# An attention and gated-MLP block on one core: loads on SP's queue, closing steps on Pool, a bf16 product with gb

## The chip, the cores and the metric

The kernel runs on one core of one Trainium2 chip. The metric is the device time of one execution in microseconds; lower is better. TensorE (PE in the profile, PEld for its weight loads), VectorE (DVE), ScalarE (ACT), GpSimd (POOL) and SyncE (SP) each work through their own list of instructions in the order in which the program gives them; they wait for each other through semaphores. DMA transfers are issued by SP, ACT or Pool.

## The reference

Two blocks with residual connections; 2048 rows, width 512, bf16 inputs.

```
mod = silu(c) @ w_mod                      # six vectors: sa, ca, ga, sb, cb, gb
h   = layernorm(x) * (1 + ca) + sa
x   = x + ga * A(h)
h   = layernorm(x) * (1 + cb) + sb
x   = x + gb * B(h)
```

A is attention: `q = h @ wq` in 32 heads of 128; keys and values come from a cache of 8 heads with 2048 positions, each shared by 4 heads of q; `softmax(q k^T / sqrt(128)) v`, and the heads' results times `wo`. B is a gated MLP: `z = gelu(h @ w_in)`; its second half is normalised by rows and mixed over positions, `g = w_sp @ z2 + b_sp`; the result is `(z1 * g) @ w_out`.

## The kernel before

**Attention.** The work is cut into 128 units (NU): 8 groups, one for each key head, by 16 tiles of 128 rows. A unit is one tile of q against one key head, for 4 heads. Group g, tile j is unit 16 g + j. The program writes the order out by hand: a loop of iterations `it` (L1404), each of 8 slots. Iteration `it` computes the scores of unit `it` (`qk`, L996), the PV products of an earlier unit and, at its end, the output projection (`wo_proj`, L1118) of a still earlier one. `at(it, slot, fn)` (L993) puts any other step in front of a given slot; `fill` holds the matmuls of the q projection for the next block of 4 units (L947). Iterations of the steady part take some 8.7 us.

**Two kinds of units.** From unit 8 to unit 118 every second unit is "by rows" (`by_rows`, L972). In a unit by columns the scores stand with the key positions on the partitions (L1030); ACT's exp (L1037) writes them so that PV can use them at once, in the next iteration (L1086, o_ps). DVE divides by the sums (L1097 and L1098, into onorm), and a DMA transpose on SP turns the result into oT (L1109). In a unit by rows the scores stand the other way (L1011); exp (L1018) writes rows into one of six buffers called pn (three of them lie in win_sb, one in wmod_a), and after each head a DMA transpose of 512 KB on SP turns that head's rows into pT (`turn_rows`, L1047, L1050): the "turns", four in such a unit, the last at slot 0 of the following iteration. PV of a unit by rows follows three iterations later (L1065, with a copy by DVE at L1074).

**The output projection** of a unit by columns runs three or four iterations after its scores (L1143, bank misc) and DVE adds it to the fp32 accumulator of its tile (xacc, L1130); a unit by rows has one matmul, one bank and one scaled addition for each head (L1136). There are two banks each of misc and o_ps; TensorE can only begin to write a bank again when DVE has read it. In the last group (units 112 to 127) each tile is closed: product with ga_rows (L1158), addition to x_sb (L1159), then bn_stats and bn_aggr (`ln_stats`, L696 to L699), all on DVE. The second LayerNorm of the tile follows (`ln2`, L1166): the reciprocal root on Pool (L679, L683), the normalisation on DVE (L687), a transpose on SP (xnT, L1177), the modulation on DVE (hT, L1184).

**Loads.** For each group g the weights wq and wo, the values v and the keys kT are loaded into buffers of which there are two each (`load_wq`, `load_v`, `load_wo`, `load_k`, L720 to L746). The keys go by a DMA transpose on SP. The other three are issued by Pool, at slot 5 of the iteration that follows a unit by rows (L1294 to L1308): in front of each load Pool copies one element of that unit's pT (`after_rows`, L1283), so it waits until the unit's last turn has landed. For group 1 the three loads stand at (5, 0) behind `after_pv(3)`. Pool also issues the rest of w_mod (wmod_b, at (2, 5)), w_in (win_sb, at (126, 4)), and w_out and b_sp at the end of iteration 130 (L1440, L1441). wmod_b is read by `mod_cols_b` (L1197, matmuls at L857) at (4, 4).

**The MLP.** From iteration 128 on, matmuls of z2 (L1321) and z1 (L1360) stand between the last PV products; then come the statistics and the normalisation of z2 on DVE (L1343, L687), the spatial product (L1486) with the w_sp tiles, loaded by DMA transposes on SP (`load_wsp`, L1216), and the product with w_out (L1519). `finish_tile` (L1527) multiplies the result with gb_rows into an fp32 tile tmp (L1531), adds x_sb into yout (L1532), and ACT issues the store (L1533).

Of the kernel before, what the change touches and what calls it, by code (L numbers as in the profile page):

```python
# [10 lines left out]
BF16 = mybir.dt.bfloat16  # L11
FP32 = mybir.dt.float32
ACT = mybir.ActivationFunctionType
ALU = mybir.AluOpType
AX = mybir.AxisListType
P = 128
# [559 lines left out]
def kernel(  # L576
# [19 lines left out]
    nc = tc.nc  # L596
    _, S, D = A_x.shape
    _, HKV, SK, DH = A_k_cache.shape
    HQ = A_wq.shape[1] // DH
    REP = HQ // HKV  # L600
    F = B_w_in.shape[1]
    FH = F // 2
    NMOD = w_mod.shape[1]
    assert DH == P and D == 512 and S % 512 == 0 and SK % 1024 == 0 and FH % P == 0 and REP == 4
    NT = S // P
    NDT = D // P
    NKT = SK // P
    NFT = FH // P
    NCH = S // 512
    CT = 512 // P  # L610
# [11 lines left out]
    v_dram = A_v_cache[0].rearrange("g (t p) d -> p g t d", p=P)  # L622
# [3 lines left out]
    wmod_dram = w_mod.rearrange("(p dt) n -> p dt n", p=P)  # L626
    c_dram = c[0].rearrange("(p j) -> p j", p=P)
    win_dram = B_w_in.rearrange("(dt p) f -> p dt f", p=P)
    wout_dram = B_w_out.rearrange("(ft p) d -> p ft d", p=P)
# [10 lines left out]
    stat = fast.enter_context(tc.tile_pool(name="stat", bufs=2))  # L640
# [7 lines left out]
    ga_rows = res.tile([P, D], FP32, name="ga_rows")  # L648
    gb_rows = res.tile([P, D], FP32, name="gb_rows")
    modc = res.tile([P, 6 * NDT], FP32, name="modc")  # L650
    rall = res.tile([P, NT * HQ], FP32, name="rall")
# [68 lines left out]
    def load_wq(g, engine):  # L720
        wqs[g] = early.tile([P, NDT, REP * DH], BF16, name="wq_g")
        engine.dma_start(
            out=wqs[g][:], in_=wq_dram[:, :, g * REP * DH : (g + 1) * REP * DH]
        )

    def load_v(g):
        v1 = late.tile([P, NKT, DV], BF16, name="v1")
        nc.gpsimd.memset(v1[:, :, DH:DV], 1.0)
        if g > 0:
            nc.gpsimd.dma_start(out=v1[:, :, 0:DH], in_=v_dram[:, g])  # L730
        else:
            nc.sync.dma_start(out=v1[:, 0 : NKT // 2, 0:DH], in_=v_rows)
            nc.sync.dma_start(
                out=v1[:, NKT // 2 : NKT, 0:DH], in_=v_dram[:, 0, NKT // 2 : NKT]
            )
        groups.setdefault(g, {})["v1"] = v1

    def load_wo(g, engine):
        wo_g = late.tile([P, REP, D], BF16, name="wo_g")
        engine.dma_start(out=wo_g[:], in_=wo_dram[:, g * REP : (g + 1) * REP, :])  # L740
        groups[g]["wo"] = wo_g

    def load_k(g):
        kT = early.tile([P, SK], BF16, name="kT")
        nc.sync.dma_start_transpose(out=kT[:], in_=A_k_cache[0, g])
        groups.setdefault(g, {})["kT"] = kT  # L746
# [218 lines left out]
    NU = HKV * NT  # L965
# [27 lines left out]
    def at(it, slot, fn):  # L993
        later.setdefault((it, slot), []).append(fn)
# [123 lines left out]
    def wo_proj(u):  # L1118
        g, j = divmod(u, NT)
        each = by_rows(u)  # L1120
        ps = {}

        def into(first, X_ps, scale):
            if first:
                xaccs[j] = late.tile([P, D], FP32, name=f"xacc{j}", bufs=1)
            xa = xaccs[j]
            if scale is None and first:
                nc.vector.tensor_copy(out=xa[:], in_=X_ps[:])
            elif scale is None:
                nc.vector.tensor_tensor(out=xa[:], in0=X_ps[:], in1=xa[:], op=ALU.add)  # L1130
            elif first:
                nc.vector.tensor_scalar(
                    out=xa[:], in0=X_ps[:], scalar1=scale, scalar2=None, op0=ALU.mult
                )
            else:
                nc.vector.scalar_tensor_tensor(  # L1136
                    out=xa[:], in0=X_ps[:], scalar=scale, in1=xa[:], op0=ALU.mult, op1=ALU.add
                )

        def mm(hh):  # L1140
            if hh == 0 or each:
                ps[0] = bank("misc")
            nc.tensor.matmul(  # L1143
                ps[0][:],
                lhsT=oTs[u][:, hh, :],
                rhs=groups[g]["wo"][:, hh, :],
                start=(hh == 0 or each),
                stop=(hh == REP - 1 or each),
            )
            if each:  # L1150
                c0 = u * REP + hh
                into(g == 0 and hh == 0, ps[0], rall[:, c0 : c0 + 1])
            elif hh == REP - 1:
                into(g == 0, ps[0], None)
            if hh < REP - 1 or g < HKV - 1:
                return
            xa = xaccs[j]
            nc.vector.tensor_tensor(out=xa[:], in0=xa[:], in1=ga_rows[:], op=ALU.mult)  # L1158
            nc.vector.tensor_tensor(  # L1159
                out=x_sb[:, j, :], in0=xa[:], in1=x_sb[:, j, :], op=ALU.add  # L1160
            )
            ln_stats(mv2, j, x_sb[:, j, :])

        return [lambda hh=hh: mm(hh) for hh in range(REP)]
# [89 lines left out]
    ln1_at(1, (0, 7), (1, 2), (2, 2))  # L1254
    ln1_at(2, (2, 4), (3, 1), (4, 5))
    ln1_at(3, (5, 1), (5, 5), (7, 4))
    at(2, 5, lambda: nc.gpsimd.dma_start(out=wmod_b, in_=wmod_dram[:, :, 2 * D : NMOD]))
    at(NU - 2, 4, lambda: nc.gpsimd.dma_start(out=win_sb, in_=win_dram))
    at(4, 4, mod_cols_b)
    at(5, 4, mod_rows)  # L1260

# [18 lines left out]
    at(NU + 1, 0, wsp0)  # L1280
    for st in range(NT):
        at(NU + 1 + st // 4, 2 * (st % 4), lambda st=st: load_wsp(wsp[0], 0, st))
    def after_rows(u):  # L1283

        seen = stat.tile([1, 1], BF16, name="seen")
        nc.gpsimd.tensor_copy(out=seen[:], in_=pTs[u][0:1, NKT - 1, 511:512])

    def after_pv(u):
        seen = stat.tile([1, 1], FP32, name="seen")
        nc.gpsimd.tensor_copy(out=seen[:], in_=rall[0:1, u * REP : u * REP + 1])  # L1290

    at(5, 0, lambda: after_pv(3))
    pauses = [u for u in row_units if not by_rows(u + 1)]
    for g in range(1, HKV):  # L1294
        it = (g - 1) * NT
        loads = (
            (0, lambda g=g: load_wq(g, nc.gpsimd)),
            (4, lambda g=g: load_v(g)),
            (6, lambda g=g: load_wo(g, nc.gpsimd)),
        )  # L1300
        last = it - 1
        for from_it, load in loads:
            if g == 1:
                at(5, 0, load)
                continue
            last = next(u for u in pauses if u >= it + from_it and u > last)
            at(last + 1, 5, lambda u=last: after_rows(u))
            at(last + 1, 5, load)  # L1308
        last = next(u for u in pauses if u >= it + 8 and u > last)
        at(last + 1, 1, lambda g=g: load_k(g))  # L1310


    zs = {}
# [90 lines left out]
    for it in range(NU + 6):  # L1404
        if it < NU:
            if it % CT == 0 and it // CT + 1 < NB:
                set_fill(it // CT + 1)
        elif it == NU:
            free_a.close()
            z2p = fast.enter_context(tc.tile_pool(name="z2p", bufs=1))  # L1410
            zs["z2"] = z2p.tile([P, NT, FH], BF16, name="z2")
        pvs = [u for u in range(max(it - 5, 0), min(it, NU)) if pv_at(u) == it]
        wos = [u for u in range(max(it - 8, 0), min(it, NU)) if wo_at(u) == it]
        wf = [fn for u in wos for fn in wo_proj(u)]
        for i in range(NSLOT):
            for fn in later.pop((it, i), []):
                fn()
            if it < NU:
                qk(it, i)
            if len(pvs) == 1:  # L1420
                pv_part(pvs[0], i, NSLOT)
            elif pvs:
                n = NSLOT // 2
                pv_part(pvs[i // n], i % n, n)
            for fn in fill.pop((it, i), []):
                fn()
            if i >= NSLOT - len(wf):
                wf[i - NSLOT + len(wf)]()
            if it >= NU:
                zrun(3)  # L1430
        for u in wos:
            if u >= (HKV - 1) * NT:
                ln2(it, u % NT)
        if it == NU + 2:
            free_b.close()
            mlp = fast.enter_context(tc.tile_pool(name="mlp", bufs=1, side="right"))
            zs["z1T"] = mlp.tile([P, NFT, S], BF16, name="z1T")
            wout_sb = mlp.tile([P, NFT, D], BF16, name="wout_sb")
            bsp_bc = mlp.tile([P, S], BF16, name="bsp_bc")
            nc.gpsimd.dma_start(out=wout_sb[:], in_=wout_dram)  # L1440
            nc.gpsimd.dma_start(out=bsp_bc[:], in_=B_b_sp.partition_broadcast(P))  # L1441
    assert not later and not fill
    for t in range(1, 3):
        wsp[t] = mlp.tile([P, NT, 512], BF16, name=f"wsp{t}")
# [81 lines left out]

    def finish_tile(t, jj, src):  # L1527
        j = t * CT + jj
        tmp = mlp.tile([P, D], FP32, name="tmp", bufs=2)
        yout = mlp.tile([P, D], BF16, name="yout", bufs=2)  # L1530
        nc.vector.tensor_tensor(out=tmp[:], in0=src, in1=gb_rows[:], op=ALU.mult)  # L1531
        nc.vector.tensor_tensor(out=yout[:], in0=tmp[:], in1=x_sb[:, j, :], op=ALU.add)  # L1532
        nc.scalar.dma_start(out=out_dram[:, j, :], in_=yout[:])  # L1533
# [84 lines left out]
```

## Time and profile before

| | us |
|---|---|
| three runs: median (lowest, highest) | 1313.51 (1313.09, 1313.7) |
| profiled execution: time | 1314.1 |
| profiled execution: span, first to last instruction | 1312.2 |
| PE busy | 1302.6 |
| ACT busy | 1111.5 |
| DVE busy | 629.5 |
| POOL busy | 55.3 |

The profile is of one execution. Its span is 1.9 us shorter than its time, and its time is 0.6 us above the median of the three runs. The granted TensorE clock was 0.999. In lists of waits the columns are: the waiting engine, line and tile, what it waited for, the total in us, how often, and the longest. In a chain and in a timeline the columns are the start in us from the start of the span, the length in us, engine, line and tile; xN stands for N merged instructions. In the table of stretches there follow, after the length, the busy time of PE, PEld, DVE, ACT and POOL with their counts, the granted clock, the share of the DMA engines and GB/s.

### The profile page before, as it was taken

To read this page: it belongs to the slowest core of one execution; us is meant where nothing else is said; L and a number is where in the kernel's file an instruction comes from. 1 tells how busy PE (TensorE), PEld (TensorE's weight loads), DVE (VectorE), ACT (ScalarE), POOL (GpSimd) and SP (SyncE) were. 2 spreads that over 40 slices of the span, in tenths; PEclk is the share of its full clock that TensorE was granted. 3 is DMA by queue.
4 is the path that set the end of the run, shared out by engine and by line. 5 is a ranking of instruction groups with operands and counts; after the bars stand their busy time and mean duration, and the time that the engine had idled before them with its cause. 6 is when DMAs were issued, how large, how long until landed. Compare 5 with 4: busy or idle time off the path is not lost.

```text
span 1312.2 us, 24106 instructions
## 1 busy us (share of the span) xinstructions
PE 1302.6 (99%) x9671; PEld 742.9 (57%) x9671; DVE 629.5 (48%) x1610; ACT 1111.5 (85%) x1509; POOL 55.3 (4%) x116
## 2 busy tenths in 40 slices
PE   9999999999999999999999999999999999999998
PEld 5665555555555555555555555555555566644445
DVE  6532444444444444444444444444444568794444
ACT  7899999999999999999999999999999988650000
POOL 1200000000000000000000000000000001120000
PEclk9999999999999999999999999999999999999999
DMA  7778878777888788787977787778876631464300
GB/s 181 152 103 153 133 141 154 137 132 140 165 154 137 141 142 156 118 145 148 167 140 130 141 158 138 129 139 168 153 137 129 115 55 30 114 139 101 74 17 31
DMA packets 584392, 168.54 MB, mean 128 GB/s; under 512 B 573936, under 2 KB 580336, under 8 KB 584272
## 3 DMA queue, kind: packets, MB, share of 16 engines
q1 hardware_dynamic: 577248, 147.77, 64.3%
q0 software_dynamic: 4432, 16.91, 4.2%
q10 hardware_dynamic: 2592, 2.23, 0.5%
q8 instruction: 78, 1.28, 0.4%
q14 instruction: 42, 0.34, 0.1%
HBM read 21.89 MB, written 2.10 MB: 18 GB/s over the span
## 4 chain that ended last, share of the span: by engine, by line
PE 97%; DMA 1%; DVE 1%; issue 0%; POOL 0%; ACT 0%; DVEq 0%
PE o_ps L1086 19%; PE s_ps L1030 18%; PE s_ps L1011 15%; PE o_ps L1065 15%; PE misc L1143 8%; PE misc L947 8%; PE misc L1486 7%; PE s_ps L1321 2%; PE s_ps L1360 2%; PE o_ps L1519 1%; DMA wsp<-in_w_mod_dram 1%; PE o_ps L788 1%; PE s_ps L1519 0%; DMA hT<-xn 0%; DVE bnst L698 0%; DVE hT L816 0%
## 5 line engine op out<-in xcount | busy, mean ns | idle before, releaser
L1037 ACT ACTIVATE pT<-s_ps 128x1024 bf16<-128x1024 f32 x552 | 561.4, 1025 | 34.6 <-PE s_ps L1030 12.3
L1086 PEld LDWEIGHTS <-pT 128*128 128x128 bf16 x4416 | 295.6, 98 | 129.8
L1030 PE MATMUL s_ps<-qT,kT 128*128 128x512 bf16 x1152 | 342.4, 379 | 0.3 <-ACT pT L1037 0.2
L1086 PE MATMUL o_ps<-v,pT 128*128 128x129 bf16 x4416 | 340.4, 220 | 0.0
L1011 PE MATMUL s_ps<-kT,qT 128*128 128x512 bf16 x896 | 266.5, 379 | 0.0
L1018 ACT ACTIVATE win_sb<-s_ps 128x1024 bf16<-128x1024 f32 x226 | 231.4, 1025 | 3.6 <-ACT win_sb L1018 0.3
L1143 PE MATMUL misc<-wo_g,oT 128*128 128x512 bf16 x512 | 194.0, 379 | 1.1 <-DVE xacc L1136 1.1
L947 PE MATMUL misc<-hT,wq_g 128*128 128x512 bf16 (+2 forms) x520 | 187.0, 371 | 0.1
L1030 PEld LDWEIGHTS <-kT 128*128 128x128 bf16 x1152 | 111.7, 98 | 115.4 <-issue 3.0
L1136 DVE SCALAR_TENSOR_TENSOR xacc<-misc,rall,xacc 128x512 f32<-128x512 f32 x220 | 163.7, 744 | 19.4 <-PE misc L1143 14.4
L958 DVE CAST qT<-misc 128x512 bf16<-128x512 f32 x125 | 85.7, 686 | 162.4 <-PE misc L947 162.4
L1018 ACT ACTIVATE pn<-s_ps 128x1024 bf16<-128x1024 f32 x148 | 151.5, 1025 | 1.6
L1065 PEld LDWEIGHTS <-v 128*128 128x128 bf16 x896 | 87.6, 98 | 105.8
L1065 PE MATMUL o_ps<-wsp,v 128*128 128x512 bf16 x448 | 133.2, 379 | 0.0
L1065 PE MATMUL o_ps<-pT,v 128*128 128x512 bf16 x448 | 132.6, 379 | 0.0
L1074 DVE CAST oT<-o_ps 128x512 bf16<-128x512 f32 x56 | 38.7, 692 | 191.5 <-PE o_ps L1065 191.5
L1011 PEld LDWEIGHTS <-qT 128*128 128x128 bf16 x896 | 87.5, 98 | 58.7
L1486 PE MATMUL misc<-wsp,z 128*128 128x512 bf16 (+2 forms) x560 | 100.7, 336 | 0.0
L1054 DVE TENSOR_TENSOR tot<-rs 128x1 f32<-128x1 f32 x224 | 34.2, 153 | 94.4 <-ACT win_sb L1018 63.0
L1486 PEld LDWEIGHTS <-z 128*128 128x128 bf16 x560 | 50.6, 98 | 48.7 <-issue 0.2
L1018 ACT ACTIVATE wmod_a<-s_ps 128x1024 bf16<-128x1024 f32 x74 | 75.8, 1025 | 0.0
L1097 DVE RECIPROCAL rall<-o_ps 128x2 f32<-128x2 f32 x144 | 24.5, 170 | 105.1 <-PE o_ps L1086 97.8
(113 smaller groups left out, 795.9 us busy)
## 6 DMA issues: line engine op xcount, KB each, us to landing
wq_g<-in_A_wq_dram POOLq DMA_DIRECT2D x7, 512.0 KB, 3.7
v<-in_A_v_cache_dram POOLq DMA_DIRECT2D x7, 512.0 KB, 5.5
wo_g<-in_A_wo_dram POOLq DMA_DIRECT2D x7, 512.0 KB, 4.3
wsp<-in_w_mod_dram POOLq DMA_DIRECT2D x1, 2048.0 KB, 11.8
out_dram<-yout ACTq DMA_DIRECT2D x16, 128.0 KB, 1.7
win_sb<-in_B_w_in_dram POOLq DMA_DIRECT2D x1, 1792.0 KB, 7.9
x_sb<-in_A_x_dram SPq DMA_DIRECT2D x3, 512.0 KB, 5.6
oT<-onorm SPq DMA_TRANSPOSE x72, 2.7
```

Of the source, the lines that this page charges most:

```text
L947: nc.tensor.matmul(ps[0][:, o0 : o0 + n], lhsT=wqs[g][:, dt, hh * DH : (hh + 1) * DH], rhs=hTs[ch][:, dt, c0 : c0 + n], start=(dt == 0), s ...
L958: nc.vector.tensor_copy(out=dst, in_=src)
L1011: nc.tensor.matmul(s_ps[:, c * 512 : (c + 1) * 512], lhsT=qTs[b][:, hh, jj * P : (jj + 1) * P], rhs=groups[g]["kT"][:, k0 : k0 + 512], sta ...
L1018: nc.scalar.activation(out=rows_of(u, hh)[:, half * HK : (half + 1) * HK], in_=s_ps[:], func=ACT.Exp, scale=inv_sqrt_dh, accum_out=rsums[u ...
L1030: nc.tensor.matmul(s_ps[:, h * 512 : (h + 1) * 512].rearrange("p (r q) -> p r q", r=REP), lhsT=groups[g]["kT"][:, kt * P : (kt + 1) * P], ...
L1037: nc.scalar.activation(out=pTs[u][:, 2 * i : 2 * i + 2, :], in_=s_ps[:].rearrange("p (k q) -> p k q", k=2), func=ACT.Exp, scale=inv_sqrt_dh,)
L1065: nc.tensor.matmul(o_pss[u][:], lhsT=groups[g]["v1"][:, kt, 0:DH], rhs=pTs[u][:, kt, :], start=(kt == 0), stop=(kt == NKT - 1),)
L1074: nc.vector.tensor_copy(out=oTs[u][:], in_=o_pss[u][:].rearrange("p (r q) -> p r q", r=REP))
L1086: nc.tensor.matmul(o_ps[:, hh % 2, 0 : DH + 1], lhsT=pTs[u][:, kt, hh * P : (hh + 1) * P], rhs=groups[g]["v1"][:, kt, 0 : DH + 1], start=( ...
L1136: nc.vector.scalar_tensor_tensor(out=xa[:], in0=X_ps[:], scalar=scale, in1=xa[:], op0=ALU.mult, op1=ALU.add)
L1143: nc.tensor.matmul(ps[0][:], lhsT=oTs[u][:, hh, :], rhs=groups[g]["wo"][:, hh, :], start=(hh == 0 or each), stop=(hh == REP - 1 or each),)
L1486: nc.tensor.matmul(g_pss[f][:, :n], lhsT=z2[:, st, f * P : (f + 1) * P], rhs=wsp[t][:, st, c0 : c0 + n], start=(st == 0), stop=(st == NT - ...
```

## The change

- The loads of wq, v and wo for groups 1 to 7 are issued by SP, at slot 1 of the iteration after a unit by rows, without the copies on Pool (`after_rows` and `after_pv` are gone). For group 1 they stand at (6, 2). The keys keep their place.
- wmod_b goes to SP at (1, 4) instead of Pool at (2, 5); win_sb to SP at (TURN_B + 1, 2), which is (120, 2), instead of Pool at (126, 4); w_out and b_sp to SP at the same place as before.
- For tiles 0 to 11 of the last group the product with ga_rows and the addition to x_sb run on Pool. `ln_stats` stays on DVE behind them.
- tmp in `finish_tile` is written and read as bf16, in the same memory.

```diff
-            nc.gpsimd.dma_start(out=v1[:, :, 0:DH], in_=v_dram[:, g])
+            nc.sync.dma_start(out=v1[:, :, 0:DH], in_=v_dram[:, g])
...
             xa = xaccs[j]
-            nc.vector.tensor_tensor(out=xa[:], in0=xa[:], in1=ga_rows[:], op=ALU.mult)
-            nc.vector.tensor_tensor(
+            engine = nc.gpsimd if j < NT - CT else nc.vector
+            engine.tensor_tensor(out=xa[:], in0=xa[:], in1=ga_rows[:], op=ALU.mult)
+            engine.tensor_tensor(
                 out=x_sb[:, j, :], in0=xa[:], in1=x_sb[:, j, :], op=ALU.add
             )
             ln_stats(mv2, j, x_sb[:, j, :])
...
-    at(2, 5, lambda: nc.gpsimd.dma_start(out=wmod_b, in_=wmod_dram[:, :, 2 * D : NMOD]))
-    at(NU - 2, 4, lambda: nc.gpsimd.dma_start(out=win_sb, in_=win_dram))
+    at(1, 4, lambda: nc.sync.dma_start(out=wmod_b, in_=wmod_dram[:, :, 2 * D : NMOD]))
+    at(TURN_B + 1, 2, lambda: nc.sync.dma_start(out=win_sb, in_=win_dram))
...
-    at(5, 0, lambda: after_pv(3))
     pauses = [u for u in row_units if not by_rows(u + 1)]
     for g in range(1, HKV):
         it = (g - 1) * NT
         loads = (
-            (0, lambda g=g: load_wq(g, nc.gpsimd)),
+            (0, lambda g=g: load_wq(g, nc.sync)),
             (4, lambda g=g: load_v(g)),
-            (6, lambda g=g: load_wo(g, nc.gpsimd)),
+            (6, lambda g=g: load_wo(g, nc.sync)),
+            (8, lambda g=g: load_k(g)),
         )
         last = it - 1
         for from_it, load in loads:
-            if g == 1:
-                at(5, 0, load)
+            if g == 1 and from_it < 8:
+                at(6, 2, load)
                 continue
             last = next(u for u in pauses if u >= it + from_it and u > last)
-            at(last + 1, 5, lambda u=last: after_rows(u))
-            at(last + 1, 5, load)
-        last = next(u for u in pauses if u >= it + 8 and u > last)
-        at(last + 1, 1, lambda g=g: load_k(g))
+            at(last + 1, 1, load)
...
-            nc.gpsimd.dma_start(out=wout_sb[:], in_=wout_dram)
-            nc.gpsimd.dma_start(out=bsp_bc[:], in_=B_b_sp.partition_broadcast(P))
+            nc.sync.dma_start(out=wout_sb[:], in_=wout_dram)
+            nc.sync.dma_start(out=bsp_bc[:], in_=B_b_sp.partition_broadcast(P))
...
-        tmp = mlp.tile([P, D], FP32, name="tmp", bufs=2)
+        tmp = mlp.tile([P, D], FP32, name="tmp", bufs=2)[:].bitcast(BF16)[:, 0:D]
```

More of the change, by code (lines that the diff above doesn't have):

```diff
@@ L1282 @@
         at(NU + 1 + st // 4, 2 * (st % 4), lambda st=st: load_wsp(wsp[0], 0, st))
[L1283 to L1290, printed above, removed]
-    at(5, 0, lambda: after_pv(3))
     pauses = [u for u in row_units if not by_rows(u + 1)]
```

## The prediction

> **What bounds the kernel.** I read the page first (busy shares and slices), then who waited for whom on TensorE, then the table of 20 us stretches, then the chain and the timelines where TensorE is not full.
>
> ```profile
> PE 1302.6 (99%) x9671; PEld 742.9 (57%) x9671; DVE 629.5 (48%) x1610; ACT 1111.5 (85%) x1509; POOL 55.3 (4%) x116
> ...
> PE   9999999999999999999999999999999999999998
> ```
>
> A busy PE is not yet PE at its peak, so I looked at its pace as well. In the chain a pair of units repeats every 17.44 us (169.33, 186.77, 204.21), each pair of 512-column matmuls takes 0.43 us and eight of 129 columns 0.45 us, and from 140 to 1080 us the starts in the timeline follow each other at that pace, without a gap. What TensorE waits for by name is nearly nothing:
>
> ```profile
> PE o_ps L788 <- DVE onorm L769: 1.2, 1, 1.2
> PE misc L1143 <- DVE xacc L1136: 1.1, 1, 1.1
> PE misc L857 <- DMA wsp<-in_w_mod_dram: 0.8, 1, 0.8
> ```
>
> So the change, which leaves every matmul as it is, can win only three things: the wait at L857 (0.9 us by the start times: the matmul before it starts at 47.99, L857 at 48.96), the wait at L1143 (1.1 us, near 1098), and the tail behind the last matmul. Loss has no such limit: whatever makes TensorE wait is added in full.
>
> **1. Loads on SP's queue: wmod_b, −0.9.** Today Pool issues it at 37.08, behind its LayerNorm steps, and it lands 11.83 us later, after L857 wants it. At slot (1, 4) on SP it stands behind four hT transposes, whose issue ends at 29.2. With the same 11.8 us it lands at 41, 7 us before 47.99. Behind it stand the first two oT transposes, issued from 29.26; 12 us late they land near 44, and L1143 first reads one at 50.66. So the 0.9 us go, and nothing is late next.
>
> **2. Loads on SP's queue: the three of each group, 0.** They move from slot 5, behind a copy that waited for the unit's last turn, to slot 1 of the same iteration, where SP has just issued that turn.
>
> ```profile
> 157.88 4.54 SPq L1050 DMA_TRANSPOSE wsp<-win_sb  x2
> 162.52 1.56 SPq L1109 DMA_TRANSPOSE oT<-onorm  x1
> 169.41 1.97 SPq L1050 DMA_TRANSPOSE pT<-win_sb  x1
> ```
>
> SP is free from 164.1 to 169.4. A load of 512 KB lands in 3.7 to 5.5 us (page, part 6). SP's own issue of it: 0.52 us for L740's wo; v has 256-byte pieces, and L733, with half as many, took 2.05 us, so some 4 us. It fits the gap, or makes the next turn a microsecond late. A turn feeds its PV only from the third iteration on, some 10 us after its own landing, so that cover takes all of it. The buffers are long free: v of group g−2 is last read four iterations before v of g is loaded, its wo three, its wq more, so SP doesn't wait for them. The removed copies and the Pool issues lie on an engine 4% busy and hid nothing. For group 1, three loads at (6, 2), near 64 us, stand in front of oT transposes read two iterations (17 us) later; at 5 us each that costs nothing.
>
> **3. win_sb, wout and bsp on SP, 0 (at most 1 to 3).** win_sb goes out near 1058; L1321 reads it at 1129.9 without a gap today, so earlier wins nothing. Its 8 us lie ahead of one xnT transpose (1061.94), whose reader on DVE runs at 1072.3. wout and bsp wait on SP for DVE's last closing (Pool issued them at 1154.83), and behind them stand three wsp transposes and the last xnT. That one went out at 1157.83 and DVE waited for it until 1163.79; I estimate 2 us more, from 1 to 1.5 us of issue and the 6.5 us of wout ahead. DVE then works without a break to 1186.97, and is wanted again at 1190.32: 3.3 us of cover.
>
> **4. bf16 product with gb, −0.3.** Only the last tile counts: the last matmul ends at 1306.2, then 0.69 (L1531), 0.69 (L1532), and the store. The first reads PSUM and keeps its 0.69. The second becomes all bf16; L1514 (gb times z1T, 128x512, all bf16) takes 425 ns instead of 692. 0.27 us go.
>
> **5. Closing steps on Pool, +2.2.** For tiles 0 to 11 the product with ga_rows and the addition (L1158, L1159) move to Pool, but bn_stats (L698), the next instruction in DVE's order, reads their result. So DVE is not relieved: it stands still while Pool works, and everything behind (qT casts, the adding of misc banks, onorm) stands with it. Today, at the place where TensorE waits:
>
> ```profile
> 1095.27 0.61 DVE xacc L1130
> ...
> 1095.90 0.70 DVE xacc L1158
> ...
> 1096.63 0.70 DVE x_sb L1159
> ...
> 1097.36 0.70 DVE bnst L698
> ...
> 1098.27 0.65 DVE xacc L1136
> ...
> 1098.95 0.38 PE misc L1143
> ```
>
> From the end of L1130 (1095.87) to bn_stats are 1.49 us. On Pool it is 2P + 0.2, with P for one operation and 0.2 for the handovers (0.09 from DVE to Pool, 0.08 between two Pool operations, 0.03 back, all from the rstd rows).
>
> No row shows P. The nearest on Pool:
>
> ```profile
> 0.24 0.10 POOL L1602 MEMSET const-float32-0.0<- 128x1 f32 x1 [0.24 <-issue]
> ...
> 0.76 0.20 POOL masks.py:197 MEMSET ident<- 128x128 bf16 x1
> 1.04 0.29 POOL masks.py:199 TENSOR_SCALAR_AFFINE_SELECT ident<-ident 128x128 bf16<-128x128 bf16 x1
> ```
>
> A column written costs 0.8 ns (0.20 less 0.10 over 127), and with one operand read 1.5. By the same step two operands give 2.2 ns, 512 columns 1.2 us. That is my value. Lower end: memset's slope alone, 0.5 us. Upper end: the power at L683 costs 0.156 us a column (128x4 1.04, 128x1 0.58), which would be 80 us; a product is no power, so I stop at twice the slope of the one-operand row, 1.6 us.
>
> The Trainium skill (GPSIMD Engine Reference, "Performance versus the Vector engine") says that a two-input elementwise operation is about twice as slow there as on VectorE, 4497 against 2293 ns for 2048 fp32. An estimate from it for 512 is 1.12 us; the stalls below would then be 1.1 us and the whole sum −0.1. No Pool row here can test it.
>
> With P = 1.2 each closing holds DVE 2.6 instead of 1.49 us: 1.1 later. What that costs is read from DVE's idle time before TensorE rewrites the bank in question:
>
> ```profile
> 1060.00:1080.00 20.00, 20.00 (x185) 12.78 (x183) 13.83 (x33) 15.40 (x16) 1.36 (x3) 1.00 0.18 27
> 1080.00:1100.00 20.00, 18.95 (x193) 12.80 (x191) 15.90 (x38) 17.49 (x18) 2.38 (x6) 1.00 0.15 27
> 1100.00:1120.00 20.00, 20.00 (x207) 13.74 (x205) 18.99 (x49) 18.87 (x20) 4.21 (x9) 1.00 0.18 35
> ```
>
> (After the stretch's length come PE, PEld, DVE, ACT and POOL; DVE is busy 13.83, 15.90 and 18.99 of 20 us.) Followed closing by closing:
> - Units 113, 115, 117: DVE idles 0.48, 0.72, 0.78 us before L1097, so 0.6, 0.4, 0.3 are left, against slacks of 0.64, 0.44, 0.44 us at the row unit's L1136 behind. They just fit: 0.1. Units 112, 114, 116 have 2 to 4 us.
> - Unit 119 (the fence above): TensorE already waits, so all of it is added: 1.1.
> - Units 118, 120, 121, 122 and 123 follow while DVE is full: five times 1.1, less 0.2 to 0.7 of idle, against 3.4 to 4.2 us from onorm (L1098) to the next use of that o_ps bank. 0.3, 0.2 and 0.4 stick out at 1117.5, 1122 and 1129.5. DVE is level again at 1138, where it idled 2.5.
>
> Sum 2.1 to 2.2. By P: 0.7 at 1.0, 0.9 at 1.1, 2.2 at 1.2, 3.9 at 1.3, 7.5 at 1.5; −0.3 at 0.5.
>
> **Sum.** −0.9 − 0.3 + 2.2 = +1.0 on the profiled execution: its span 1312.2 becomes 1313.2, its time 1314.1 becomes 1315.1. It is 0.6 above the median of the three runs; on that median, 1313.5, the forecast is 1314.5. About 0.2% (2.6 us) is what a measurement can tell from no change, so this is "within".
>
> **Rivals.**
> - *DVE becomes the bound* (slower). Same mechanism, P of 1.3 or more: from there the stalls are 3.9, the sum passes +2.7, and each further 0.1 us of P costs 1.8. At 1.4: 1318.0. For it: the fixed cost of a Pool operation with a column operand is 0.23 (L679), not 0.10, and the second has mixed types. Against it: the slope above. Chance 0.25.
> - *SP's queue becomes a wait*: wout and bsp make the last xnT over 3.3 us late, or a load pushes a turn past its 10 us of cover. Price, at 5 us late, 1.7 us once: 1316.2; three late loads in each of 7 groups at 0.3 us: 1320. For it: SP's q1 carries 64.3% already. Against: the gaps above. Chance 0.1, half of it over the bound.
> - *Pool is cheap* (P from 0.5 to 1.0): the stalls are −0.3 to 0.7 and the sum −1.5 to −0.5: 1312 to 1313. Chance 0.2, within the bound.
> - *The kernel is faster by over 2.6*: all that TensorE waits from 20 us on adds to some 3 us, a third of it where ACT is full (80 to 130). It would need a gain that I don't see. Chance 0.05.
> - The forecast itself (P from 1.0 to 1.3, queues silent): 0.4.
>
> Faster 0.05, within 0.65, slower 0.30. The range reaches from the cheap Pool, 1312.2, to P = 1.4, 1318.0.
>
> **What would show it.** Pool rows at L1158 and L1159's new places near 1.2 us, and DVE's bn_stats waiting for Pool 12 times; L1143's wait near 1098 at 2.2 instead of 1.1; new waits of L1086 on onorm between 1115 and 1135; no L857 wait; the last yout at 0.43. TensorE still without a gap from 140 to 1030. The prediction fails if a gap stands there, if the first mm of the spatial stage waits for DVE, or if P is outside 1.0 to 1.3.

## The result, and the profile after

The changed kernel takes 1315.95 us (median of 15 runs, 1315.6 to 1316.64) against 1313.51 (15 runs, 1312.62 to 1314.39): ratio 1.0019, 95% interval 1.0011 to 1.0027, so 1.4 to 3.5 us slower. The interval leaves out "no change", and the forecast of +1.0 lies below it. The time lies inside the predicted range and the ratio just inside the 0.2% that the prediction counts as "within"; its value was 1.45 us low. The profiled execution of after took 1315.95 us with a span of 1313.8, 1.6 more than the span before.

The lines of the page that answer to those shown of before:

```profile
PE 1303.2 (99%) x9671; PEld 743.0 (57%) x9671; DVE 606.4 (46%) x1586; ACT 1111.4 (85%) x1509; POOL 59.0 (4%) x96
...
PE   9999999999999999999999999999999999999998
...
q1 hardware_dynamic: 601200, 164.16, 69.2%
```

DVE lost 23 us of work (mostly the 24 operations that went to Pool, and some 4 us by step 4) and the kernel became slower: DVE's busy time was not what counted. What TensorE waits for by name (the list of waits, TensorE's lines):

```profile
PE misc L1143 <- DVE xacc L1136: 2.2, 1, 2.2
PE o_ps L788 <- DVE onorm L769: 1.2, 1, 1.2
PE s_ps L1030 <- ACT pT L1037: 1.0, 2, 0.7
PE o_ps L1086 <- DVE onorm L1098: 0.4, 2, 0.3
```

L1143's wait has doubled, L857's is gone, and two kinds are new or larger: L1086 behind onorm (forecast) and L1030 behind ACT's exp (not forecast). I then put the starts of all matmuls of both traces side by side and took as lost what lies between two starts above the usual pace. The place of a gap is the last start before it. In us of the span:

| stretch | before | after | where |
|---|---|---|---|
| 0 to 20 | 4.4 | 4.6 | start of the program |
| 20 to 60 | 0.9 | 0 | L857, at 48 |
| 60 to 80 | 0 | 0.9 | L1030, at 71.5 |
| 80 to 140 | 1.3 | 1.3 | the same places |
| 140 to 1040 | 0 | 0 | |
| 1040 to 1160 | 1.2 | 3.3 | after, at 1098: 2.34; 1118.6: 0.42; 1123.5: 0.23; 1131.2: 0.35 |
| last matmul's start to the end | 6.4 | 5.7 | tail |

The differences add to 0.2 − 0.9 + 0.9 + 2.1 − 0.7 = 1.6; the spans differ by 1.6.

The largest item is the closing step. The two new groups on Pool (shapes kept apart; busy us and mean ns behind the first bar):

```profile
L1159 POOL TENSOR_TENSOR xacc<-xacc,ga_rows 128x512 f32<-128x512 f32 x12 | 15.2, 1269 | 218.4 <-DVE xacc L1130 201.5 <-DVE xacc L1136 16.9
L1160 POOL TENSOR_TENSOR x_sb<-xacc,x_sb 128x512 bf16<-128x512 f32 x12 | 13.9, 1156 | 0.9
```

And the chain at the place that the prediction showed (start, length, what):

```profile
1095.50 0.61 DVE xacc L1130
1096.10 0.07 issue
1096.17 1.28 POOL xacc L1159
1097.45 0.07 issue
1097.52 1.16 POOL x_sb L1160
1098.68 0.02 issue
1098.71 0.71 DVE bnst L698
1099.41 0.02 issue
1099.44 0.18 DVE mv L699
1099.62 0.65 DVE xacc L1136
```

From the end of L1130 to bn_stats are 2.6 us instead of 1.49; L1136, which frees the bank for L1143, comes 1.1 us later. The list of waits counts DVE's standing still:

```profile
DVE bnst L698 <- POOL x_sb L1160: 31.4, 12, 2.6
```

The stretches show the same from above (length; then PE, PEld, DVE, ACT, POOL):

```profile
1060.00:1080.00 20.00, 20.00 (x184) 12.81 (x183) 11.55 (x30) 15.40 (x16) 5.43 (x9) 1.00 0.34 95
1080.00:1100.00 20.00, 18.13 (x185) 12.35 (x184) 12.00 (x32) 17.44 (x18) 7.72 (x10) 1.00 0.14 27
1100.00:1120.00 20.00, 19.43 (x196) 13.24 (x196) 11.52 (x32) 17.79 (x18) 9.50 (x12) 1.00 0.11 22
```

DVE's busy time falls from 15.90 to 12.00 and from 18.99 to 11.52, and TensorE's falls with it, from 18.95 to 18.13 and from 20.00 to 19.43. A part of the fall is the work that went to Pool; but DVE also stands behind Pool, 2.6 us in each closing, so a lower busy share here does not mean room.

SP's queue carries the group loads without harm to the turns. SP's timeline of after, at the place that the prediction showed:

```profile
157.86 4.82 SPq L1050 DMA_TRANSPOSE wsp<-win_sb  x2
162.77 1.24 SPq L1109 DMA_TRANSPOSE oT<-onorm  x1
164.06 0.57 SPq L722 DMA_DIRECT2D wq_g<-in_A_wq_dram  x1
169.64 1.70 SPq L1050 DMA_TRANSPOSE pT<-win_sb  x1
```

### The profile page after: what moved, and what is told of

It is laid out like the page before. It is cut to its first block, busy times and chain, and to the rows that moved or that the text cites. A ratio compares the mean times of both kernels' runs of the same rounds, so it can differ in the third digit from the quotient of the medians.

```text
span 1313.8 us, 24042 instructions
## 1 busy us (share of the span) xinstructions
PE 1303.2 (99%) x9671; PEld 743.0 (57%) x9671; DVE 606.4 (46%) x1586; ACT 1111.4 (85%) x1509; POOL 59.0 (4%) x96
## 4 chain that ended last, share of the span: by engine, by line
PE 97%; DVE 1%; POOL 1%; issue 0%; ACT 0%; DVEq 0%; POOLq 0%
PE o_ps L1086 19%; PE s_ps L1030 18%; PE s_ps L1011 15%; PE o_ps L1065 15%; PE misc L947 8%; PE misc L1143 8%; PE misc L1475 7%; PE s_ps L1310 2%; PE s_ps L1349 2%; PE o_ps L1508 1%; PE o_ps L788 1%; POOL xacc L1159 0%; PE s_ps L1508 0%; POOL x_sb L1160 0%; DVE bnst L698 0%
## 5 line engine op out<-in xcount | busy, mean ns | idle before, releaser
L1086 PEld LDWEIGHTS <-pT 128*128 128x128 bf16 x4416 | 295.6, 98 | 130.5 <-issue 1.0
L1030 PE MATMUL s_ps<-qT,kT 128*128 128x512 bf16 x1152 | 342.4, 379 | 1.1 <-ACT pT L1037 1.0
L1086 PE MATMUL o_ps<-v,pT 128*128 128x129 bf16 x4416 | 340.4, 220 | 0.4 <-DVE onorm L1098 0.4
L1143 PE MATMUL misc<-wo_g,oT 128*128 128x512 bf16 x512 | 194.0, 379 | 2.2 <-DVE xacc L1136 2.2
L1030 PEld LDWEIGHTS <-kT 128*128 128x128 bf16 x1152 | 111.6, 98 | 117.4 <-issue 5.2
L1136 DVE SCALAR_TENSOR_TENSOR xacc<-misc,rall,xacc 128x512 f32<-128x512 f32 x220 | 163.5, 743 | 19.6 <-PE misc L1143 14.6
```

The source lines that it names most:

```text
L1030: nc.tensor.matmul(s_ps[:, h * 512 : (h + 1) * 512].rearrange("p (r q) -> p r q", r=REP), lhsT=groups[g]["kT"][:, kt * P : (kt + 1) * P], ...
L1086: nc.tensor.matmul(o_ps[:, hh % 2, 0 : DH + 1], lhsT=pTs[u][:, kt, hh * P : (hh + 1) * P], rhs=groups[g]["v1"][:, kt, 0 : DH + 1], start=( ...
L1136: nc.vector.scalar_tensor_tensor(out=xa[:], in0=X_ps[:], scalar=scale, in1=xa[:], op0=ALU.mult, op1=ALU.add)
L1143: nc.tensor.matmul(ps[0][:], lhsT=oTs[u][:, hh, :], rhs=groups[g]["wo"][:, hh, :], start=(hh == 0 or each), stop=(hh == REP - 1 or each),)
```

## The experiments

Every edit is shown against the kernel that it starts from. Ratios are to the kernel before on the same chip, with 95% intervals; its medians there were 1313.19 to 1314.2 us. "Gap" is the excess of one start-to-start distance of matmuls over their pace.

**closings_only: before, with step 5 alone.**

```diff
-            nc.vector.tensor_tensor(out=xa[:], in0=xa[:], in1=ga_rows[:], op=ALU.mult)
-            nc.vector.tensor_tensor(
+            engine = nc.gpsimd if j < NT - CT else nc.vector
+            engine.tensor_tensor(out=xa[:], in0=xa[:], in1=ga_rows[:], op=ALU.mult)
+            engine.tensor_tensor(
```

> The kernel before with one edit: the closing steps of tiles 0 to 11 on Pool. My theory (DVE stands still behind bn_stats): all of the slowdown is here. +2.1 us over before, L1143's wait near 1098 at 2.2 to 2.3 us instead of 1.1, some 1.0 us of waits for o_ps between 1115 and 1135, no other new gap on TensorE. Rival A (the loads on SP's queue cost, Pool's closing is hidden by the banks): within 0.5 us of before.

Measured: 1317.28 us, ratio 1.0030 (1.0018 to 1.0043), +3.8 us: more than the whole change. The gaps of after are all there, to 0.02 us (2.34, 0.42, 0.24, 0.35), and one more, of 1.67 us at 1131.5. Pool's issue of w_in in the kernel before, and then, of this kernel, Pool's timeline and what waits at 1133:

```profile
1118.88 0.83 POOL L1258 DMA_DIRECT2D win_sb<-in_B_w_in_dram  x1 [0.19 <-ACT wsp L1037]
...
1119.21 1.26 POOL L1159 TENSOR_TENSOR xacc<-xacc,ga_rows 128x512 f32<-128x512 f32 x1 [3.67 <-DVE xacc L1130]
1120.55 1.16 POOL L1160 TENSOR_TENSOR x_sb<-xacc,x_sb 128x512 bf16<-128x512 f32 x1
...
1123.80 0.83 POOL L1259 DMA_DIRECT2D win_sb<-in_B_w_in_dram  x1 [0.19 <-issue]
...
1133.20 0.74 PE L1322 MATMUL s_ps<-win_sb,hT 128*128 128x448 bf16 x3 [1.51 <-DMA win_sb<-in_B_w_in_dram]
```

The load now stands behind two closings and the reciprocal roots that wait for them, and goes out 4.9 us later, and the first matmul of z2 (L1322 here) waits for it. So in this change SP's early issue of win_sb is worth 1.7 us, because step 5 makes Pool late.

**loads_only: after, with the closing steps back on DVE** (steps 1 to 4 alone).

```diff
-            engine = nc.gpsimd if j < NT - CT else nc.vector
-            engine.tensor_tensor(out=xa[:], in0=xa[:], in1=ga_rows[:], op=ALU.mult)
-            engine.tensor_tensor(
+            nc.vector.tensor_tensor(out=xa[:], in0=xa[:], in1=ga_rows[:], op=ALU.mult)
+            nc.vector.tensor_tensor(
```

> The changed kernel with the closing steps back on DVE: the moved loads and the bf16 product alone. My theory: -1.2 us against before (the wait at L857, 0.9, and 0.3 in the tail), waits at 1098 as before (1.1). Rival A (the loads on SP's queue cost something that the profile of the changed kernel shows as 0.9 us without a named cause at 71.5 us, while group 1's three loads are in flight): that gap is here again and the time is -0.3 us. Rival B (the gap belongs to one execution): it is not here.

Measured: 1313.49 us, ratio 1.0000 (0.9991 to 1.0009). No wait at L857, the gap at 1098 is 1.21 as in before, the tail 5.7, and a gap of 1.53 us at 71.4 takes the gain away. The forecast −1.2 did not come: something in steps 1 to 4 costs about what they win.

**stats_later: after, with bn_stats of tiles 0 to 11 at slot 2 of the next iteration**, so that other work of DVE can stand in front of it.

```diff
-            ln_stats(mv2, j, x_sb[:, j, :])
+            if j >= NT - CT:
+                ln_stats(mv2, j, x_sb[:, j, :])
...
-        at(it + 1, 0, first)
-        at(it + 1, 4, second)
+        if j < NT - CT:
+            at(it + 1, 2, lambda: ln_stats(mv2, j, x_sb[:, j, :]))
+            at(it + 1, 3, first)
+            at(it + 1, 6, second)
+        else:
+            at(it + 1, 0, first)
+            at(it + 1, 4, second)
```

> The changed kernel with bn_stats and bn_aggr of tiles 0 to 11 two slots into the next iteration, so that DVE has other work while Pool closes a tile; the steps behind them move with them (rstd to slot 3, normalisation to slot 6). My theory: the same Pool operations cost nothing once DVE does not stand behind them; all waits of TensorE between 1040 and 1140 go, also the 1.1 us of the kernel before. -2.3 us against before, some -4.5 against the changed kernel. Rival (Pool's operations slow DVE by themselves, through a shared way to the memory, or the delayed LayerNorm is late for z2): no gain, or DVE's operations beside Pool's are longer than 0.69 us (1136: longer than 0.74).

Measured: 1311.98 us, ratio 0.9989 (0.9980 to 0.9998), 4.0 us below after. From 1040 to 1160 one gap of 0.14 us is left; the kernel before's own 1.21 us at 1098 is gone with the others. Pool does the same 24 operations for the same time. The rival, Pool slowing DVE by itself, holds for one kind of operation: L1136 beside Pool takes 0.75 us as elsewhere, but four of the modulations (hT, 0.30 us elsewhere) last 1.15 to 1.27 us, each beginning 0.05 to 0.11 us behind a Pool operation and ending 0.05 us behind it. TensorE loses nothing there. And DVE has not stopped standing behind Pool:

```profile
DVE bnst L698 <- POOL x_sb L1160: 22.3, 10, 2.6
```

In ten of the twelve closings bn_stats still waits for Pool, 22.3 us in all instead of 31.4 in after. In the first six hardly anything of DVE's stands between, and DVE idles 2.3 to 2.6 us as in after; TensorE waited for none of this in after either. Near 1098 two of L1136 now come first and bn_stats waits only 0.7 us, and in the five closings after that DVE stands 6.2 us instead of 13.1. So the edit did not end the standing; it took it away where TensorE waited for what stands behind bn_stats.

**third_pool_op: after, with a third operation of the same size on Pool in each closing**, a sum into a tile that nobody reads.

```diff
+            if j < NT - CT:
+                junk = late.tile([P, D], BF16, name="junk", bufs=1)
+                engine.tensor_tensor(out=junk[:], in0=xa[:], in1=x_sb[:, j, :], op=ALU.add)
```

> The changed kernel with one more Pool operation of the same size in each closing of tiles 0 to 11 (a sum into a tile that nobody reads), between the two. By the bookkeeping of DVE's idle time and slack, a closing of 3.9 instead of 2.6 us costs 13 us over before, 11 over the changed kernel: now units 113, 115 and 117 stick out too, 1.6 to 2 us each. Rival (only unit 119, where TensorE already waits, counts): +1.2 us over the changed kernel.

Measured: 1327.17 us, ratio 1.0103 (1.0088 to 1.0119); 11.2 us above after, for 12 operations of 1.16 us. Its waits of TensorE:

```profile
PE o_ps L1086 <- DVE onorm L1098: 4.7, 3, 2.0
PE misc L1143 <- DVE xacc L1136: 3.8, 3, 3.4
PE misc L1143 <- DVE qT L958: 2.1, 3, 0.9
```

The slack that swallowed the first 1.1 us in the early units is used up: TensorE now waits at three places there too, but 1.1 to 1.2 us each, where 1.6 to 2 were expected of units 113, 115 and 117. What TensorE loses from 1040 to 1160 adds to 14.9 us instead of 3.3, which is 11.6 more for a dose of 13.9 us. Not all of it is waiting: TensorE stands still 3.57 us at L1143, up to 1104.74, and the granted clock is 0.50 from 1103.5 to 1110.3 us, where matmuls of 512 columns start 0.43 us apart instead of 0.21. That costs 2.7 of the 14.9 us; the waits add to 12.2, 8.9 more than in after. In no other run does the clock fall between the first 8 us and the tail.

**wmod_only: before, with step 1 alone.**

```diff
-    at(2, 5, lambda: nc.gpsimd.dma_start(out=wmod_b, in_=wmod_dram[:, :, 2 * D : NMOD]))
+    at(1, 4, lambda: nc.sync.dma_start(out=wmod_b, in_=wmod_dram[:, :, 2 * D : NMOD]))
```

> The kernel before, with wmod_b alone issued by SP at slot (1, 4) instead of by Pool at (2, 5). Theory (step 1 of the prediction stands by itself): the gap of 0.9 us at L857 is gone, nothing else is late, 0.9 us less than before. Rival (the gap near 71 us is only L857's gap come back later, in whatever kernel loses the wait at L857): L857 runs without a wait and a gap of about 0.9 us stands near 71 us at L1030, though group 1's loads are still on Pool; 0.0 us.

Measured: 1313.06 us, ratio 0.9998 (0.9989 to 1.0007). No wait at L857 near 48 us and no gap near 71, so the rival (L857's gap come back) fell. But 0.9 us are not won by the medians either: 0.1 us less, and the interval reaches from 1.4 less to 0.9 more, so it does not exclude them.

**group1_only: before, with group 1's three loads alone on SP at (6, 2)**, and without Pool's copy in front of them.

```diff
-            nc.gpsimd.dma_start(out=v1[:, :, 0:DH], in_=v_dram[:, g])
+            (nc.sync if g == 1 else nc.gpsimd).dma_start(out=v1[:, :, 0:DH], in_=v_dram[:, g])
...
-    at(5, 0, lambda: after_pv(3))
...
-            (0, lambda g=g: load_wq(g, nc.gpsimd)),
+            (0, lambda g=g: load_wq(g, nc.sync if g == 1 else nc.gpsimd)),
...
-            (6, lambda g=g: load_wo(g, nc.gpsimd)),
+            (6, lambda g=g: load_wo(g, nc.sync if g == 1 else nc.gpsimd)),
...
-                at(5, 0, load)
+                at(6, 2, load)
```

> The kernel before, with group 1's three loads alone (wq, v, wo) issued by SP at (6, 2), and the copy on Pool that waited for the third unit left out. Theory (these loads at this place delay ACT's exp near 71 us by themselves): the gap of 0.9 us at L857 stays and one of 0.9 to 1.5 us stands near 71 us; 0.9 to 1.5 us more than before. Rival (the gap near 71 us is L857's come back): L857's gap stays, none near 71 us; 0.0 us.

Measured: 1314.07 us, ratio 1.0007 (0.9998 to 1.0016). The gap near 71 us is there, 0.54 us at 70.7, though nothing else of the change is in this kernel. Its size is below the expected 0.9, and the median's +0.9 is not told from zero. Moving the loads brings the gap without any other part of the change; and the theory's other half, that L857's gap stays, failed: L857 did not wait at 48 us in this execution, with wmod_b on Pool as in before.

**bf16_only: before, with step 4 alone.**

```diff
-        tmp = mlp.tile([P, D], FP32, name="tmp", bufs=2)
+        tmp = mlp.tile([P, D], FP32, name="tmp", bufs=2)[:].bitcast(BF16)[:, 0:D]
```

> The kernel before, with the product with gb kept in bf16 alone. Theory (step 4): the last addition takes 0.42 instead of 0.69 us, the span 0.3 us less. Rival (the tail of 6.4 us became 5.7 in every kernel with the whole change, so more than the addition is shorter): 0.7 us less, with the store's way to the end 0.4 us shorter too.

Measured: 1313.48 us, ratio 1.0002 (0.9993 to 1.0011), too small to be seen in the time. The last addition takes 0.43 us instead of 0.69. The tail is 6.35 us against 6.4, and the two kernels above, which lack this step, have 6.0 and 6.5: the store's end scatters by more than the step is worth, so the tail's −0.7 in after is not all step 4's.

**group1_later and group1_pool: loads_only, with group 1's loads elsewhere**, spread over three later iterations on SP, or on Pool at (5, 0) as before.

```diff
-            if g == 1 and from_it < 8:
-                at(6, 2, load)
+            if g == 1:
+                at(*{0: (9, 2), 4: (11, 1), 6: (13, 1), 8: (9, 1)}[from_it], load)
```

> The kernel of loads_only (moved loads and bf16 product, closing steps on DVE) with group 1's three loads still on SP, but one at a time behind units by rows, at (9, 2), (11, 1) and (13, 1), as the other groups have them. loads_only stands still at 71.4 us (L1030, 1.5 us) while three loads follow each other in SP's queue. Theory (three loads at once, in the stage in which the fill of the LayerNorm and of the mod rows is still going on, hold up the queue and what TensorE and ACT exchange): the gap goes, -1.3 against loads_only and before, no gap at the new places. Rival (any load directly behind transposes in SP's queue does it): gaps of about a microsecond at 90, 107 and 125 us.

Measured: 1312.36 us, ratio 0.9990 (0.9981 to 0.9999). The gap at 71.7 is down to 0.48, not to zero.

```diff
-            nc.sync.dma_start(out=v1[:, :, 0:DH], in_=v_dram[:, g])
+            (nc.gpsimd if g == 1 else nc.sync).dma_start(out=v1[:, :, 0:DH], in_=v_dram[:, g])
...
+    at(5, 0, lambda: after_pv(3))
...
-                at(6, 2, load)
+                at(5, 0, load)
```

(and wq and wo in the same way.)

> The kernel of loads_only with group 1's three loads back on Pool at (5, 0) behind the copy, as before the change; all other loads stay on SP. Theory (SP's queue at (6, 2) is what stands still at 71.4 us): the gap goes, -1.3 against loads_only and before. Rival (the gap comes from something else of the early stage that the change moved, such as wmod_b): the gap stays near 70 us, and the time is that of loads_only.

Measured: 1313.12 us, ratio 0.9995 (0.9986 to 1.0004). No gap at 71, but TensorE waits 0.6 us for ACT at 85.1 instead. The three intervals (with loads_only's) overlap, so the times alone do not rank the places; the gaps do only for 71 us.

**closings_win_early: closings_only, with win_sb issued by Pool at (120, 2).**

```diff
-    at(NU - 2, 4, lambda: nc.gpsimd.dma_start(out=win_sb, in_=win_dram))
+    at(TURN_B + 1, 2, lambda: nc.gpsimd.dma_start(out=win_sb, in_=win_dram))
```

> The kernel of closings_only with win_sb issued by Pool at (120, 2) instead of (126, 4). In closings_only L1322 waited 1.5 us for win_sb: Pool issued it at 1123.8 instead of 1118.9, behind the rstd steps of tiles that DVE closes late. Theory: that wait goes and 2.1 us of the closing steps stay, +2.1 against before. Rival (the wait for win_sb only uncovers another one, such as hT or a full queue): +3.8 as in closings_only.

Measured: 1315.74 us, ratio 1.0017 (1.0008 to 1.0026), 2.1 above before; the wait for win_sb is gone and the four gaps of the closings stay (2.34, 0.41, 0.23, 0.35). So step 5 by itself costs 2.1, as its gaps say, and the other 1.7 of closings_only was the late load.

**stats_later_g1_later: both remedies together** (the edits of stats_later and group1_later).

> The kernel of stats_later with group 1's loads as in group1_later: what the two findings give together. Theory: all named waits after 20 us are gone; -2.3 to -2.6 against before, and 0.2 to 1 under stats_later, whose own gap at 71.7 us was only 0.16 in its profile. Rival (the gap at 71 us costs nothing outside the profiler): the same as stats_later, -1.5.

Measured: 1311.46 us, ratio 0.9981 (0.9972 to 0.9990): faster than both kernels, 2.15 us below before and 4.5 below after. What is left of the gap near 71 is 0.28.

**stats_later_dve: the same, with all closing steps back on DVE.**

```diff
-            engine = nc.gpsimd if j < NT - CT else nc.vector
+            engine = nc.vector
```

> stats_later_g1_later with the closing steps of all tiles back on DVE: the statistics stay one iteration later. Theory (the gain of that kernel comes from the later place of bn_stats, not from Pool): of the 1.2 us that TensorE waits at L1143 near 1098 in the kernel before, bn_stats and bn_aggr (0.9 us) no longer stand in front of L1136, so 0.3 us are left; elsewhere between 1040 and 1160 nothing new; time 0.3 us above stats_later_g1_later, 2.1 us less than before less 0.3. Rival (Pool's relief is what makes room where DVE is full, near 1117 to 1131): the 1.4 us of the two operations come back there as stalls, gaps of 0.3 to 1 us at several places and 1 to 3 us above stats_later_g1_later, no longer faster than before.

Measured: 1311.92 us, ratio 0.9982 (0.9973 to 0.9991). Its timeline at the place of the chain above:

```profile
1094.79 0.68 DVE L1130 TENSOR_TENSOR xacc<-misc,xacc 128x512 f32<-128x512 f32 x1
...
1095.50 0.69 DVE L1159 TENSOR_TENSOR xacc<-xacc,ga_rows 128x512 f32<-128x512 f32 x1
...
1096.23 0.69 DVE L1160 TENSOR_TENSOR x_sb<-xacc,x_sb 128x512 bf16<-128x512 f32 x1
...
1096.84 1.60 DVE L1136 SCALAR_TENSOR_TENSOR xacc<-misc,rall,xacc 128x512 f32<-128x512 f32 x2
...
1097.63 0.38 PE L1143 MATMUL misc<-wo_g,oT 128*128 128x512 bf16 x1
```

L1136 follows the closing at once, bn_stats comes at 1098.35, and the gap at L1143 is 0.29 instead of 1.21 us: the expected 0.3. Behind it one of 0.11 is left and no other from 1040 to 1160, though DVE is busy 18.74 of 20 us from 1100 to 1120. The rival fell: even where DVE is full, Pool's help buys 0.3 us by the gaps (0.14 are left with it, 0.40 without). The times show no gain: each against the kernel before on its own chip, this kernel is 2.28 us below and the one with Pool's help 2.15.

## Why the prediction came out as it did

**Step 5 (Pool's closing steps, +2.2) was right, in cause, places and size.** P was put at 1.2 us from the slope of Pool's own rows; it is 1.27 and 1.16, mean 1.21. That it came out so near is luck in part: the slope was carried from 128 columns with at most one operand to 512 columns with two, and no Pool row bore on that. The gaps grew by 2.1 us, and the four places are those of the forecast: L1143 near 1098, then 1118.6, 1123.5 and 1131.2 against 1117.5, 1122 and 1129.5, with 0.42, 0.23 and 0.35 against 0.3, 0.2 and 0.4. Units 113, 115 and 117 just fitted, as worked out. The price list by P was tried with a third operation: it says 1.8 us for each further 0.1 us of P, and a third operation is like 0.6 us more on each of the two, so 11 us. 11.2 came, but that they agree so well is luck: 2.7 us of it are the slower clock, the waits grew by 8.9, and what they would have been at full clock no run shows. That the cause is DVE standing behind Pool with TensorE's work behind it, and not Pool's work itself, is shown by stats_later: there the same Pool operations cost TensorE 0.14 us, although DVE still stands 22.3 us at places where TensorE has cover. The Trainium skill (GPSIMD Engine Reference, "Performance versus the Vector engine") gives 4497 ns for 2048 fp32, an estimate of 1.12 us here; the trace is 13% and 3% above that for the two forms, and against DVE's 0.70 the operations are 1.8 and 1.7 times as long, where the page says about twice.

**Step 1 (wmod_b, −0.9) failed in size: it was read from one execution.** The wait at L857 near 48 us is gone in all nine profiled kernels that issue wmod_b on SP. But of the five that leave it on Pool, the wait stands in two (before 0.91, closings_only 0.62) and in three it is absent (closings_win_early, group1_only, bf16_only). Its mean over the five is 0.3 us; I take that as the step's gain, an estimate from five single executions. wmod_only's 0.1 fits it but does not exclude 0.9. Where before's profile said 0.8 for one wait, I took a size that scatters as if it were fixed.

**Step 2 (the group loads) was right for groups 2 to 7 and failed for group 1: "at 5 us each that costs nothing".** From 140 to 1040 us TensorE has no gap in any of the kernels. SP's issue of v took 0.53 us, not the 4 that I feared. But near 71 us ACT begins an exp late. ACT's timeline of before there, without a break, and then the timeline of after (SPq is SP's issue, with the time in which the issue stood):

```profile
61.98 18.64 ACT L1037 ACTIVATE pT<-s_ps 128x1024 bf16<-128x1024 f32 x17
...
68.48 7.76 SPq L740 DMA_DIRECT2D wo_g<-in_A_wo_dram  x1
...
71.46 0.38 PE L1143 MATMUL misc<-wo_g,oT 128*128 128x512 bf16 x1
71.51 1.94 ACT L1037 ACTIVATE pT<-s_ps 128x1024 bf16<-128x1024 f32 x2 [1.48 <-PE s_ps L1030]
72.04 0.58 POOL L1214 DMA_DIRECT2D ga_rows<-mod  x1 [10.78 <-DMA mod<-modc]
72.58 0.59 PE L1030 MATMUL s_ps<-qT,kT 128*128 128x512 bf16 x2 [0.75 <-ACT pT L1037]
```

ACT idles 1.48 us in front of an exp whose scores TensorE, by the profile's modelled ends, had finished at 70.07, and TensorE then waits for ACT. I had followed whom the three loads delay in SP's queue (the oT transposes) and not looked for another way to reach ACT. The gap stands in all five profiled kernels with these loads at (6, 2): 0.91, 1.53, 0.95, 0.54 and 0.16 us, mean 0.8; none stands there in the six that leave them on Pool. That the move of these loads brings it is shown by group1_only, and by the count, with one profile for each kernel. The move has two halves, off Pool and onto SP at this place. The three kernels that have the loads off Pool but later on SP (group1_later, stats_later_g1_later, stats_later_dve) keep 0.48, 0.28 and 0.37 us, so the place is not all of it.

How they reach ACT stays open. The trace's semaphore records narrow it down: TensorE's semaphore, for which this exp waits, was raised at 71.49, 0.02 us before the exp began. In all five kernels with the loads at (6, 2) the exp follows such a late update by 0.02 us. So ACT was not slow to start; TensorE's signal came 1.4 us after the modelled end of the scores. (One update that the exp at 69.00 must have had is not recorded, so the records are incomplete there.) The DMA records show long packets at the same time: packets of 256 bytes on q1, which take 0.02 us in the middle, took up to 3.8 us there (30 of them over 1 us); in before the longest is 1.3 us. From 69.0 to 71.2 us no packet of q1 starts; but in before none starts from 71.3 to 75.3, and there TensorE loses nothing, so the pause alone explains nothing. Pool's write of mod to DRAM in pieces of 4 bytes is under way there in all kernels. No load of instructions for an engine falls into that time. But ACT's exp reads and writes no tile that a DMA touches then, and a part of the gap stays without the loads. Nothing tried here separates the write, the transposes and the loads.

**Step 3 (win_sb, wout and bsp, 0) was right as the sum stands, and wrong in its reason for win_sb.** "L1321 reads it without a gap today, so earlier wins nothing" costed the edit against the kernel before; with step 5 the load would have come late on Pool, and SP's early issue saves 1.7 us. The two errors cannot be seen in after, since both parts are in it. wout and bsp cost nothing, as forecast, but the 2 us that I estimated for the last xnT did not come: it went out 3.8 us later than in before, 1.5 more than TensorE's own delay of 2.3, and landed faster; DVE waited 1.18 us for it, until 1164.55, where it had waited 2.53. The spatial stage begins without a gap.

**Step 4 (bf16 product, −0.3)** was right in the instruction, 0.42 us for 0.69. The time cannot show it.

**The sum.** With the terms as the runs give them, 2.1 (step 5) + 0.8 (group 1) − 0.3 (wmod_b) − 0.3 (bf16) = +2.3; measured +2.4 (1.4 to 3.5). The two small terms are means of a few profiles that scatter by several tenths, so that the sum closes to 0.1 is luck in part. The forecast +1.0 lacked the gap at 71 us and took the one at 48 us three times too large. That the time still fell into the range is owed to the width left for P; the two terms that missed had none. (By the price list the low end is 1312.0, at P = 0.5, and not 1312.2.) Of the rivals, "SP's queue becomes a wait" comes nearest: loads on SP did bring a wait, but at a place and on an engine that it did not name, in a way that is not shown, and at half its price.

## What to carry to other kernels

An operation moved to a slower engine does not relieve the first engine if that engine's next instruction reads the result: it stands still for the whole detour, and its busy time falls while the kernel gets slower. Look first for the reader and move it behind what a full engine is waiting for; here this won nearly all there was, and the move to the other engine then added 0.3 us at most: it took some 17 us of work off DVE (24 times 0.69) and made it stand 22.3. Standing still where the full engine has cover cost nothing. Cost each edit with the others in place, since a queue that one edit slows may hold what another edit takes out of it, and take a wait's size from more than one execution before counting its removal as a gain.

## What the runs showed of the hardware beyond the forecast

Three direct loads of 512 KB on SP, issued behind five transposes while a write in pieces of 4 bytes was under way, came with single packets of q1 that lasted up to 3.8 us in after; TensorE's signal for an exp on ACT that needs none of that data came 0.7 us (stats_later) to 2.0 us (loads_only) after the scores' modelled end. The way from one to the other is not shown. Away from such a place SP issues such a load in 0.5 to 0.6 us, also with pieces of 256 bytes.

An all-bf16 operation of DVE on 128x128 elements (hT, in stats_later), which takes 0.30 us by itself, lasted 1.15 to 1.27 us each of the four times that it began during Pool's 128x512 products and sums, and ended 0.05 us behind them; L1136, with fp32 operands, kept its 0.75 us beside them.

In third_pool_op TensorE stood still for 3.57 us before 1104.74, and its granted clock read 0.50 from 1103.5 to 1110.3 us; around the waits of 2.34 us in after and 2.17 us in third_pool_op it stayed at 1.00.
